# Masked queries on VectorE alone, and feature-map exponentials given to ScalarE only when their buffer is free

## The chip, the cores and the metric

The kernel runs on one core of a Trainium2 chip, as one launch. The metric is the device time of that launch in microseconds (us), the median of several runs. The core has five engines that each work through their own queue of instructions in order and wait for each other by semaphores: PE (TensorE, matrix multiply), DVE (VectorE), ACT (ScalarE), POOL (GpSimd) and SP (SyncE, which here only issues DMAs).

## The reference

A residual stream `x` of 2048 tokens by 512 features in bfloat16 goes through four layers, A, B, A, B. Each layer adds its output to `x`:

```
x = x + A(layernorm(x));  x = x + B(layernorm(x));  x = x + A(layernorm(x));  x = x + B(layernorm(x))

A: q, k, v = x@wq, x@wk, x@wv           32 heads of 16, 4 segments of 512 tokens
   for each segment s:
     a_dot = softmax(q_s k_s^T * 0.25 + causal mask) v_s
     pq    = phi(q_s);  a_mem = pq M / (pq z + 1e-6)
     o_s   = g * a_mem + (1 - g) * a_dot          g = sigmoid(beta)
     M, z += phi(k_s)^T v_s, sum(phi(k_s))        phi(t) = t + 1 where t > 0, else exp(t)
   return o @ wo
B: q, k, v = split(x @ wqkv);  return softmax(q k^T * 0.25) v @ wo       32 heads of 16, all 2048 tokens
```

Layer B's attention has 32 heads x 2048 x 2048 scores, each of which needs an exponential; there are two such layers. Layer A's is within segments and causal, and adds two feature maps `phi` per segment.

## The kernel before, in words

**An order written at build time.** A Python class (`Builder`) runs once when the program is built. It keeps a planner (`Sched`) with a clock for each engine, `sc.t[...]`. Each instruction that is added gets a planned end from a duration and a rate in its call (`ns`, `gap`), and semaphore waits are worked out from what it reads and writes. The planner's clocks decide what is added next, so a changed duration or engine changes the order of everything after it. On the chip nothing is decided: each engine executes its list in order.

**Steps.** The main loop (`attention`) is a series of steps (1407 before the change). A step takes three banks of scores (`take_banks`): a bank is 128 keys by 512 queries of one head, one bank of PSUM. `unit` adds the PE matmuls that make the scores, and one ACT instruction (L1289) that exponentiates all three banks, 1,536 columns wide, from PSUM into `pT` in SBUF. Two sets of three PSUM banks alternate. Two steps later `pv_step` multiplies `pT` with the values into an accumulator in PSUM bank 6. When a group of banks is done (one half of the heads of a 128-feature chunk, for one segment of queries), `finish` has DVE divide by the sums (L1341, a reciprocal, and L1349, which writes `ob`); PE can't start the next group's accumulation before that.

**Exponentials on DVE.** `dx_pick` takes some banks out of layer B's groups. Their scores go to PSUM bank 7; DVE copies and scales them (`dx_first`, L932), and a chain of five DVE instructions for a pair of banks (`dx_chain`, L957 to L968) makes the exponential with integer and float16 arithmetic into `dxo` (some of the tiles lie in `KA`, `QA` and `VA`, once these are no longer needed). A bank is picked only if the planner's DVE clock isn't too late.

**Background.** Everything else (layer norm, projections, memory, output projections) is written as generators ("tasks"). Each `yield` names what must be met (a flag, a DMA landed, a step reached), and the PE and DVE time of what follows; `background` runs what fits between steps. `keep_busy` adds dummy matmuls with zero weights where PE has little to do.

**Masked queries.** Heads have 16 features, and the score matmuls contract over 32 rows, so that two heads share a row block. For each group the queries are multiplied with a column of zeros and ones that keeps one head of the two: `qm = q * par` (`select`, L1197, 128 x 512 bfloat16). There are six `qm` buffers. The engine is chosen by

```
eng = "dve" if late or isA or any(h.kind == "A" for h in self.sel) else "pool"
```

so POOL makes those of layer B when the group is selected ahead of time and no layer-A group is selected: 86 of 160. They are made in pairs (the two groups of a chunk), normally when the second group of the pair before begins.

**Feature maps.** `phi(src, ...)` takes `[128 x 1024]` of keys or queries at a time. ACT writes `exp(src)` into the buffer `amem` (L618, 24 times), and two steps later or more DVE does `max(src, 0) + 1` (L620) and the minimum of that and `amem` (L621). There is one such buffer, which the memory part also uses (L707 writes it, and a DMA transpose reads it). In the kernel before nothing in the planner holds the ACT instruction back: it is added as soon as the task comes to it, and ACT's queue waits there on a semaphore until the minimum of the call before has read `amem`.

Of the kernel before, what the change touches and what calls it, by code (L numbers as in the profile page):

```python
# [23 lines left out]
LAG = {"pe": 100, "act": 60, "dve": 60, "pool": 70, "sp": 50}  # L24
# [231 lines left out]

class Builder:
    NPU = 4
    LAG_M = 2
    LOOK, PV_TAKEN = 1, 1  # L260
    NQM = 6
# [26 lines left out]
    def alloc(self):  # L288
# [21 lines left out]
        self.rd = sb("rd", [P, 2, 16], f32)  # L310
        self.pT = sb("pT", [P, self.NPU, 3, 512], bf)
        self.qm = sb("qm", [P, self.NQM, 512], bf)
# [44 lines left out]
        self.b_rd = n1("rd", 2)  # L357
        self.b_pT = n1("pT", self.NPU * 3)
        self.b_qm = n1("qm", self.NQM)
# [255 lines left out]
    def phi(self, src, bsrc, dst, bdst):  # L615

        et = self.amem[:, :, :, :].rearrange("p a b c -> p a (b c)")
        self.op("act", lambda e: e.activation(et, src, ACT.Exp), reads=bsrc, writes=self.b_amem, ns=1023, gap=915)  # L618
        yield [("at", self.step + 2)], 0, 1130
        self.op("dve", lambda e: e.tensor_scalar(dst, src, 0.0, 1.0, op0=ALU.max, op1=ALU.add), reads=bsrc, writes=bdst, ns=430)  # L620
        self.op("dve", lambda e: e.tensor_tensor(dst, dst, et, ALU.min), reads=self.b_amem + bdst, writes=bdst, ns=690)  # L621
# [392 lines left out]
    def met(self, need):  # L1014
        def done(key):
            step, end = self.dma_at.get(key, (-9, 0.0))
            return self.bubble or self.forcing or self.step >= step + self.DMA_STEPS and end < self.sc.t["pe"] + self.DMA_LATE

        def ok(n):
            if n == "xT":  # L1020
                return len(self.xT_free) > 0
            if n == "xn":
                return done(("xn", self.rr.get("xn", 0) % 2))
            if n[0] == "dma":
                return n[1] in self.dma_at and done(n[1])
            if n == "pair":
                return len(self.dx_pairs) > 0
            if n == "slot":
                return len(self.dx_free) > 0
            if n[0] == "at":  # L1030
                return self.bubble or self.forcing or self.step >= n[1]
            return n == "cont" or n in self.flags
        return all(ok(n) for n in need)
# [124 lines left out]
    def select(self, late):  # L1158
        tail = self.sel[-2:]
        if not self.LOOK and len(self.sel) > 2 and self.seqA and self.seqA[0][0].L and all(g.kind == "B" and not g.pos for g in tail) and self.met(self.group_needs(self.seqA[0][0])):  # L1160

            for g in tail:
                self.sel.remove(g)
                self.qm_free.insert(0, g.qm)
            self.seqB.insert(0, tail)
        while len(self.qm_free) > 1:
            pair = None
            look = self.LOOK and self.wide

            at = next((i for i, g in enumerate(self.sel) if g.kind == "B" and g.e == 0 and not g.pos), len(self.sel)) if look else len(self.sel)  # L1170
            few = at <= 1 or not look and at == 2 and all(g.kind == "B" and g.total < 64 for g in self.sel)
            short = look and len(self.sel) == 2 and all(g.kind == "B" and g.total < 64 for g in self.sel)
            if self.seqA and (few or short) and self.met(self.group_needs(self.seqA[0][0])):
                pair = self.seqA.pop(0)
                if not few:
                    at = len(self.sel)
            elif self.seqB and at == len(self.sel) and (few or short or look and self.seqB[0][0].total == 64 and all(g.kind == "A" for g in self.sel)) and self.met(self.group_needs(self.seqB[0][0])):
                pair = self.seqB.pop(0)
                at = len(self.sel)
            elif short and self.seqB and self.met(self.group_needs(self.seqB[0][0])):  # L1180
                pair = self.seqB.pop(0)
                at = len(self.sel)
            elif not few and not short:
                return
            if pair is None and self.seqB and sum(len(g.banks) - g.pos for g in self.sel) <= 6 and self.split():
                pair = self.seqB.pop(0)
            if pair is None:
                return
            for i, g in enumerate(pair):
                g.qm = self.qm_free.pop(0)  # L1190
                isA = g.kind == "A"
                q = (self.QA[:, self.aslot(g.L, g.qseg), g.c, :] if isA else self.QB[:, g.qseg, g.c, :])
                bq = (self.b_QA[self.aslot(g.L, g.qseg)][g.c] if isA else self.b_QB[g.qseg][g.c])
                m = self.qm[:, g.qm, :]
                col = self.par[:, g.e:g.e + 1]
                eng = "dve" if late or isA or any(h.kind == "A" for h in self.sel) else "pool"
                self.op(eng, (lambda m, q, col: lambda e: e.tensor_scalar(m, q, col, 0.0, op0=ALU.mult, op1=ALU.add))(m, q, col),  # L1197
                        reads=[bq, self.b_par], writes=[self.b_qm[g.qm]], ns=690 if eng == "pool" else 345, gap=650 if eng == "pool" else 260)
                self.sel.insert(at + i, g)
# [26 lines left out]
    def unit(self, n, items, dx):  # L1226
        u = n % 2
        al = self.new_alloc()
        slot = n % self.NPU
        entries, first_mm, second_mm = [], [], [[], [], []]  # L1230
        for i, (g, (what, r)) in enumerate(items):
# [21 lines left out]
            if what == "k2":  # L1253

                self.held.append((n + self.LAG_M, g.mate, "k2m", r, slot, i, width))
                if r == 3:
# [274 lines left out]
```

## Time and profile before

| | |
|---|---|
| median of 3 runs (lowest, highest) | 1989.19 us (1988.31, 1990.08) |
| the profiled execution's own time | 1988.43 us |
| its span, first to last instruction | 1986.6 us |
| busy: ACT, PE, DVE, POOL | 1932.9, 1750.7, 1654.1, 88.8 us |
| ACT exponentials of scores (L1289) | 1407, 1904.6 us |
| masked queries on POOL / on DVE (L1197) | 86, 81.2 us / 74, 22.9 us |
| exponentials of feature maps (L618) | 24, 26.2 us |
| mean granted TensorE clock | 0.996 |

Busy time is the union of an engine's instructions; an instruction's recorded duration overlaps the next one's by some tens to hundreds of nanoseconds, so busy time divided by the count is what one more instruction costs an engine that is never idle. "Idle before" is idle time of an engine just ahead of a group of instructions, with what ended most of it.

### The profile page before, as it was taken

How to read it: one execution, taken by the hardware profiler on the slowest of the kernel's cores; microseconds unless marked ns; L12 is line 12 of the kernel's file. 1: busy time of each engine (PE TensorE's matmuls, PEld its weight loads, DVE VectorE, ACT ScalarE, POOL GpSimd, SP SyncE). 2: the span in 40 equal slices, each digit the busy share in tenths (PEclk: the TensorE clock that was granted, in tenths of full speed). 3: DMA queues.
4: the chain of work that ended last, by engine and by line, in shares of the span. 5: the costliest groups of instructions: out<-in, count | busy, mean ns of one | idle time of the engine just before them, and what ended most of it. 6: DMA issues, size and time to landing. Idle time of an engine off the chain costs nothing.

```text
span 1986.6 us, 62277 instructions
## 1 busy us (share of the span) xinstructions
PE 1750.7 (88%) x27733; PEld 934.8 (47%) x27733; DVE 1654.1 (83%) x2960; ACT 1932.9 (97%) x1447; POOL 88.8 (4%) x132
## 2 busy tenths in 40 slices
PE   8998898888888888888888889988888888888888
PEld 5554454444554445444454445544444444444444
DVE  5655554599899998899879996489999999999997
ACT  7899999999999999999999999999999999999998
POOL 0000001100010000000000000001000000000000
PEclk9999999999999999999999999999999999999999
DMA  5211111000000001100101011000000000000000
GB/s 155 36 21 34 28 21 26 4 10 18 16 10 15 5 15 21 18 15 5 18 19 16 5 24 22 15 5 7 15 5 4 5 15 5 5 7 14 6 5 12
DMA packets 100942, 34.82 MB, mean 18 GB/s; under 512 B 93504, under 2 KB 100160, under 8 KB 100672
## 3 DMA queue, kind: packets, MB, share of 16 engines
q1 hardware_dynamic: 100672, 30.83, 8.0%
q8 instruction: 217, 3.56, 0.8%
q14 instruction: 53, 0.43, 0.1%
HBM read 6.30 MB, written 2.10 MB: 4 GB/s over the span
## 4 chain that ended last, share of the span: by engine, by line
ACT 54%; issue 22%; PE 16%; DVE 8%; DMA 1%; SPq 0%; ACTq 0%; POOL 0%; DVEq 0%; POOLq 0%
ACT pT L1289 53%; PE ps L400 16%; ACT amem L618 1%; DVE dxo L968 1%; DMA oT<-ob 1%; DVE ob L1349 1%; DVE dxt L932 1%; DVE VA L960 0%; DVE dxz L960 0%; DVE VA L957 0%; DVE rd L1341 0%; DVE dxz L957 0%; DVE KA L932 0%; DVE phq L621 0%; DVE VB L427 0%
## 5 line engine op out<-in xcount | busy, mean ns | idle before, releaser
L1289 ACT ACTIVATE pT<-ps 128x1536 bf16<-128x1536 f32 x1407 | 1904.6, 1628 | 34.2 <-PE ps L400 31.1
L400 PE MATMUL ps<-qm,KB 32*128 32x512 bf16 x4096 | 524.8, 386 | 171.0 <-ACT pT L1289 143.1
L400 PEld LDWEIGHTS ps<-VB,pT 128*128 128x128 bf16 x14316 | 460.4, 96 | 297.4 <-issue 217.4
L400 PE MATMUL ps<-VB,pT 128*128 128x34 bf16 (+1 forms) x14316 | 576.4, 186 | 20.9 <-DVE ob L1349 12.1
L400 PEld LDWEIGHTS ps<-qm,KB 32*128 32x128 bf16 x4096 | 133.9, 91 | 498.1 <-ACT pT L1289 443.5
L400 PE MATMUL ps<-wB,zero 128*128 128x512 bf16 x1079 | 343.7, 380 | 0.0
L932 DVE TENSOR_SCALAR dxt<-ps 128x512 uint32<-128x512 f32 x260 | 178.1, 685 | 21.0 <-PE ps L400 16.5
L1197 POOL TENSOR_SCALAR qm<-QB,par 128x512 bf16<-128x512 bf16 x86 | 81.2, 946 | 1745.0 <-PE ps L400 1463.8
L400 PE MATMUL ps<-qm,KA 32*128 32x128 bf16 (+2 forms) x1536 | 86.7, 254 | 25.3 <-ACT pT L1289 22.4
L400 PE MATMUL ps<-VB,dxo 128*128 128x51 bf16 (+1 forms) x1552 | 102.7, 186 | 0.9 <-DVE dxo L968 0.7
L400 PE MATMUL ps<-VA,pT 128*128 128x51 bf16 (+1 forms) x2560 | 101.0, 187 | 2.6 <-DVE ob L1349 2.0
L400 PEld LDWEIGHTS ps<-VA,pT 128*128 128x128 bf16 x2560 | 91.9, 96 | 10.8 <-DVE ob L1349 5.5
L932 DVE TENSOR_SCALAR KA<-ps 128x512 uint32<-128x512 f32 x128 | 87.7, 685 | 9.8 <-PE ps L400 7.6
L932 DVE TENSOR_SCALAR QA<-ps 128x512 uint32<-128x512 f32 x129 | 88.5, 686 | 8.0 <-PE ps L400 6.2
L400 PE MATMUL ps<-tri,ident 128*128 128x256 bf16 (+1 forms) x640 | 94.1, 255 | 0.0
L960 DVE TENSOR_TENSOR dxz<-dxz 128x1024 f16<-128x1024 f16 (+1 forms) x131 | 89.5, 683 | 0.7
L964 DVE TENSOR_TENSOR dxz<-dxz 128x1024 f16<-128x1024 f16 (+1 forms) x131 | 89.2, 681 | 0.4
L960 DVE TENSOR_TENSOR VA<-VA 128x1024 f16<-128x1024 f16 (+1 forms) x131 | 88.4, 675 | 0.6
L964 DVE TENSOR_TENSOR VA<-VA 128x1024 f16<-128x1024 f16 (+1 forms) x131 | 88.4, 675 | 0.5
L968 DVE SCALAR_TENSOR_TENSOR dxo<-dxt,dxz 128x1024 int16<-128x1024 uint16 (+1 forms) x66 | 80.6, 1221 | 0.2
L400 PEld LDWEIGHTS ps<-qm,KA 32*128 32x128 bf16 x1536 | 38.6, 92 | 88.6 <-ACT pT L1289 48.8
L968 DVE SCALAR_TENSOR_TENSOR dxo<-dxt,VA 128x1024 int16<-128x1024 uint16 (+1 forms) x66 | 78.7, 1192 | 0.2
(125 smaller groups left out, 1625.9 us busy)
## 6 DMA issues: line engine op xcount, KB each, us to landing
out_dram<-x SPq DMA_DIRECT2D x8, 256.0 KB, 2.1
x<-in_A_x_dram SPq DMA_DIRECT2D x3, 512.0 KB, 8.6
wB<-in_B_wqkv_dram SPq DMA_DIRECT2D x1, 1536.0 KB, 12.7
oT<-ob SPq DMA_TRANSPOSE x63, 2.5
xT<-xn SPq DMA_TRANSPOSE x60, 2.4
x<-in_A_x_dram SPq DMA_DIRECT2D x4, 128.0 KB, 2.2
wA<-in_A_wk_dram SPq DMA_DIRECT2D x1, 512.0 KB, 4.1
wA<-in_A_wq_dram SPq DMA_DIRECT2D x1, 512.0 KB, 5.4
```

What stands on the lines that cost most here:

```text
L400: self.sc.add("pe", lambda e: e.matmul(out, lhsT, rhs, start=start, stop=stop, skip_group_check=True), reads=reads, banks=[(bank, "w", all ...
L618: self.op("act", lambda e: e.activation(et, src, ACT.Exp), reads=bsrc, writes=self.b_amem, ns=1023, gap=915)
L932: self.op("dve", lambda e: e.tensor_scalar(d, o, SCALE * LOG2E * 65536, 126.0 * 65536, op0=ALU.mult, op1=ALU.add), writes=self.dx_writes(" ...
L960: self.op("dve", lambda e: e.tensor_tensor(z, z, z, ALU.mult), reads=bz, writes=bz, ns=ns[0])
L964: self.op("dve", lambda e: e.tensor_tensor(z, z, z, ALU.mult), reads=bz, writes=bz, ns=ns[0])
L968: self.op("dve", lambda e: e.scalar_tensor_tensor(ob, hi, 128.0, z, op0=ALU.mult, op1=ALU.add), reads=bt + bz, writes=self.dx_writes("out" ...
L1197: self.op(eng, (lambda m, q, col: lambda e: e.tensor_scalar(m, q, col, 0.0, op0=ALU.mult, op1=ALU.add))(m, q, col), reads=[bq, self.b_par] ...
L1289: self.sc.add("act", (lambda dst, src: lambda e: e.activation(dst, src, ACT.Exp, scale=SCALE))(dst, src), writes=self.b_pT[slot * 3 + i:sl ...
L1349: self.op("dve", lambda e: e.tensor_tensor(ob, src[:, :, 0:16], rb, ALU.mult), reads=[br] + bsrc, writes=[self.b_ob[oi][g.e]], bank=bk, al ...
```

## The change

Two edits, on otherwise the same code. First, `select` gives all masked queries to DVE: the 86 that POOL made move there, and the planner now charges them to its DVE clock (its choice of `ns` and `gap` by engine stays in the line). POOL keeps the set-up and 32 small memsets. Second, `phi` gets a new `yield` ahead of the ACT instruction: the task waits until all that read or last wrote `amem`, and what last wrote the source, is planned to end no later than 40 ns after the planner's ACT clock (`LAG["act"]` is 60, `PHI_LATE` 100); DMAs among these are not counted. While it waits, the next tasks and steps go on being added.

```
 class Builder:
     NPU = 4
+    PHI_LATE = 100
...
     def phi(self, src, bsrc, dst, bdst):

         et = self.amem[:, :, :, :].rearrange("p a b c -> p a (b c)")
+        yield [("free", self.b_amem, bsrc)], 0, 0
         self.op("act", lambda e: e.activation(et, src, ACT.Exp), reads=bsrc, writes=self.b_amem, ns=1023, gap=915)
         yield [("at", self.step + 2)], 0, 1130
...
+            if n[0] == "free":
+                used = [o for b in n[1] for o in b.reads.values()] + [b.last_write for b in n[1] + n[2] if b.last_write is not None]
+                return self.bubble or self.forcing or all(o.is_dma or o.end + LAG["act"] < self.sc.t["act"] + self.PHI_LATE for o in used)
...
-                eng = "dve" if late or isA or any(h.kind == "A" for h in self.sel) else "pool"
+                eng = "dve"
                 self.op(eng, (lambda m, q, col: lambda e: e.tensor_scalar(m, q, col, 0.0, op0=ALU.mult, op1=ALU.add))(m, q, col),
                         reads=[bq, self.b_par], writes=[self.b_qm[g.qm]], ns=690 if eng == "pool" else 345, gap=650 if eng == "pool" else 260)
```

Because the planner's clocks change, the order changes too. Counted in the two built programs: the score exponentials on ACT go from 1406 of 1,536 columns and one of 512 to 1408 of 1,536 and one of 1,024; the banks that DVE exponentiates go from 517 to 510; `keep_busy` matmuls from 1079 to 1080; the DMAs stay at 195.

## The prediction

> **What bounds the kernel now.** I read the engines' busy times first, then what ACT waited for, then ACT by stage, then the rows of the moved work.
>
> From the page: the engines, and the costliest groups.
>
> ```profile
> PE 1750.7 (88%) x27733; PEld 934.8 (47%) x27733; DVE 1654.1 (83%) x2960; ACT 1932.9 (97%) x1447; POOL 88.8 (4%) x132
> ...
> L1289 ACT ACTIVATE pT<-ps 128x1536 bf16<-128x1536 f32 x1407 | 1904.6, 1628 | 34.2 <-PE ps L400 31.1
> ...
> L1197 POOL TENSOR_SCALAR qm<-QB,par 128x512 bf16<-128x512 bf16 x86 | 81.2, 946 | 1745.0 <-PE ps L400 1463.8
> ```
>
> ACT is busy for all but 1986.6 - 1932.9 = 53.7 us of the span. One exponential of three banks costs it 1904.6 / 1407 = 1.354 us; the recorded 1.628 overlaps the next. POOL has 86 masked queries and hardly anything else.
>
> What ACT waited for:
>
> ```profile
> ACT pT L1289 <- PE ps L400: 31.1, 61, 1.7
> ...
> ACT amem L618 <- DVE phk L621: 1.9, 2, 1.3
> ...
> ACT amem L618 <- DVE phq L621: 1.7, 2, 1.4
> ```
>
> Waits for the feature maps' buffer are 3.6 us, in four places. Three stand together, in ACT's timeline from 195 to 208 us (start, duration, and in brackets the idle time before):
>
> ```profile
> 196.95 1.06 ACT L618 ACTIVATE amem<-phk 128x1024 bf16<-128x1024 bf16 x1 [1.28 <-DVE phk L621]
> ...
> 201.26 1.06 ACT L618 ACTIVATE amem<-QA 128x1024 bf16<-128x1024 bf16 x1 [0.57 <-DVE phk L621]
> ...
> 206.39 1.06 ACT L618 ACTIVATE amem<-QA 128x1024 bf16<-128x1024 bf16 x1 [1.39 <-DVE phq L621]
> ```
>
> Busy time by stage (DVE, ACT and POOL are the third to fifth pair):
>
> ```profile
> 130.00:290.00 160.00, 140.94 (x2150) 79.63 (x2148) 84.70 (x198) 155.94 (x119) 9.40 (x20) 1.00 0.16 26
> 290.00:1300.00 1010.00, 892.80 (x14227) 486.10 (x14223) 835.64 (x1514) 991.45 (x738) 43.83 (x68) 0.99 0.08 15
> 1300.00:1978.00 678.00, 592.46 (x9532) 293.74 (x9530) 652.49 (x1034) 676.48 (x504) 32.18 (x26) 1.00 0.03 7
> ```
>
> So ACT idles 4.1 us from 130 to 290 (3.2 of it the waits above), 18.6 us up to 1300, 1.5 us after that, where DVE is at 96% too. What is left lies before 130 us and after 1978 us, where the change alters nothing: the first POOL query starts at 131 us, and the two programs add the same work in the same order up to step 115 (at 197 us). Hence the time moves only by ACT's own work and by those three stretches.
>
> **1. ACT's work.** The planner gives DVE seven exponential banks fewer, 510 for 517, and ACT gets them: two more instructions of three banks, 2 x 1.354 = 2.7 us, and the last, partial one has two banks for one, (1.354 - 0.49) / 2 = 0.43 us with 0.49 as the one-bank row's 0.765 us less its measured overlap. Sum **+3.1 us**, with nothing to hide it, ACT being the bound. Every other ACT count is the same.
>
> **2. The waits for `amem`.** In the order before, these four exponentials are added in the very step of the minimum (L621) that frees the buffer. In the new order the three at 197 to 206 us come one, one and two steps after it, so one, one and two ACT instructions of 1.354 us lie between; the waits were 1.28, 0.57 and 1.39. I take **-3.2 us**. The fourth (0.30 us at 109 us) is unchanged, so it stays. Bounds: -3.2, and 0 if PE can't bring the scores sooner. I take the first: PE is 88% busy there (140.94 of 160) and its waits for ACT show that it is ahead. The other exponentials come up to 16 steps later than before; the DVE minimum, the memory matmuls and their DMA transposes behind them come later with them, and the count of steps that ran short of ready banks is 54 for 55, so no attention work starves.
>
> **3. The queries on DVE.** The nearest row is the same operation there, 64 of layer A's:
>
> ```profile
> L1197 DVE TENSOR_SCALAR qm<-QA,par 128x512 bf16<-128x512 bf16 x64 | 19.7, 350 | 0.9 <-ACT QA L425 0.8
> ```
>
> 19.7 / 64 = 0.308 us, times 86 = +26.5 us of DVE. Against that, seven banks fewer: each is 0.685 us (L932) and half a chain, (0.685 + 0.689 + 0.418 + 0.687 + 1.229) / 2 = 1.85, together 2.54, so -17.8 us. And DVE loses what POOL costs it now. Of the 143 DVE instructions that overlapped one of POOL's queries, the excess over their groups' medians is 4.1 us in all, for instance here, where this form's mean is 1.230:
>
> ```profile
> 1541.69 1.63 DVE L968 SCALAR_TENSOR_TENSOR dxo<-dxt,dxz 128x1024 int16<-128x1024 uint16 x1
> ```
>
> Net +26.5 - 17.8 - 4.1 = **+4.6 us of DVE**, of some 330 us in which it idles. Does it wait for the `qm` buffer, with all of DVE's queue behind it? The 74 that DVE makes already waited 0.9 us in all, none of it on PE. In time the term is nothing by cover: what hides it is that PE runs ahead of ACT, one set of three PSUM banks. That cover is thin at one place, the end of a group:
>
> ```profile
> PE ps L400 <- DVE ob L1349: 14.1, 26, 1.5
> ```
>
> PE waits there for DVE to empty the accumulator, and where it waits 0.8 us or more, ACT idles after it. After 1300 us only the 0.98 us wait there cost ACT anything (0.45 us); four of about 0.51 and one of 0.74 cost nothing. A pair of queries (0.62 us of DVE) now stands two or three steps ahead of nearly every first end of a pair of groups, some 43 times. Bounds: +43 x 0.62 = +26.7 us if each passes through to ACT, and -4.1 us if the stretching by POOL was what held it up. I take **0**, nearest to what the order shows: in the three steps up to a group's end after step 195, the new order has 5.3 DVE instructions where the old has 5.4, since the planner charges the queries and gives something else up. I keep -4.1 for the low end, and a third of 26.7, about +9, for the high one, since the planner puts two thirds of such load elsewhere: net 4.6 of 26.5 is even less.
>
> Here the Trainium skill ("SBUF — State Buffer", section "SBUF: two separate sides") has a rule: VectorE and GpSimd take a shared port pair as an exclusive lock for a whole instruction, and the loser fully blocks. If every POOL query had blocked DVE for its shortest recorded time, 0.692 us, DVE would gain 86 x 0.692 = 59.5 us. The trace shows 4.1 on DVE and 81.2 - 59.5 = 21.7 us of stretching on POOL, so by the trace POOL is mostly the loser, and the sum keeps 4.1.
>
> **4. A forced chain.** One more group ends with its DVE exponentials not yet made (two times for once, at step 941), so that PE waits for one or two chain instructions of 0.7 to 1.2 us. The one before, near 1146 us, was followed by no ACT gap over 0.2 us. I take **+0.3**, bounds 0 and +1.5.
>
> **Sum:** +3.1 - 3.2 + 0 + 0.3 = +0.2 us. The profiled execution took 1988.43 us, 0.76 below the median of its runs; it becomes 1988.6, and the median 1989.19 becomes **1989.4 us**. A measurement of this kernel can tell about 0.2%, 4 us, from no change.
>
> **The rivals.**
> *Same, by cancelling (the forecast), chance 0.50.* +3.1 of exponentials against -3.2 of waits. Within it lies the case that the wait only changes its name, from `amem` to PE: -3.2 becomes 0, +3.4, 1992.6.
> *Group ends hold ACT up (slower), 0.27.* The 0.62 us ahead of a group's end passes the PSUM cover. Price: 0.62 us for each end that lets it through. With the +0.2 it is over 4 us from the seventh of 43 on (0.2 + 7 x 0.62 = 4.5); a third of them gives +9, 1998. For it: DVE at 96% after 1300 us, where the number of DVE banks from step 950 on is the same as before (243) and 24 queries come on top. Against it: the order's counts in part 3, and the waits of 0.51 us that cost nothing.
> *DVE is freed from POOL, and the reshuffled middle packs better (faster), 0.23.* The 4.1 us come off DVE just ahead of group ends, and come off ACT's 18.6 us of idle time between 290 and 1300. Price: -4.1, so +0.2 - 4.1 = -3.9, 1985.3; another 2 us of the 18.6 gives 1983. For it: ACT gaps at 406.6, 1043, 1077, 1126 and 1427 us stand about 6.5 us behind a pair of POOL queries. Against it: so does the end of a group anyway, and POOL pairs at 1345 and 1445 us have no gap behind them.
> By the lock rule of "SBUF — State Buffer" alone DVE would win 59.5 us, which would point to this rival; its trace price is the 4.1.
> *The change doesn't do what it says* isn't one: the order of the new program has no query on POOL, and the exponentials are moved.
>
> **How the numbers follow.** The order of everything after 197 us is reshuffled, and ACT's 20 us of idle time there is made of some 40 gaps of about half a microsecond; a few more or fewer make 2 to 4 us. Hence 0.50 within 4 us of no change, 0.27 above, 0.23 below. The range reaches to the group-end case's +9, 1998, and the packing case's 1983, and leaves about 0.1 out on either side; the likeliest case's own range is 1985.5 to 1993.
>
> **What would show it.** Right: ACT's L1289 at 1409 instructions and about 1907.7 us; no wait of L618 on L621 near 200 us, one of 0.3 near 109; POOL with 50 instructions; L1197 on DVE at 160 and about 49 us; DVE some 5 us busier, with no stretched L968. Wrong on the slow side: PE's wait for `ob` well above 14.1 us with ACT's wait for PE above 31.1. Wrong on the fast side: both below. A second way to be wrong: ACT's wait for PE grows by 3 us just where `amem`'s is gone.

## The result and the profile after

The changed kernel takes **2000.95 us** (median of 4 runs, 1997.29 to 2005.84); the kernel before, beside it, 1988.75. The ratio is 1.0058, with a 95% interval of 1.0044 to 1.0073: some 12 us slower, where 1989.4 us and no change were forecast. The profiled execution is the slowest of the four, 2005.84 us with a span of 2003.9, 17.3 us over the span before.

The engines, and the exponentials' row, in the page of the changed kernel (L1294 is the former L1289):

```profile
PE 1703.7 (85%) x27315; PEld 934.5 (47%) x27734; DVE 1655.6 (83%) x3029; ACT 1937.2 (97%) x1449; POOL 8.7 (0%) x46
...
L1294 ACT ACTIVATE pT<-ps 128x1536 bf16<-128x1536 f32 x1409 | 1909.2, 1633 | 50.3 <-PE ps L401 48.1
```

ACT does 4.3 us more, and the other 13.0 us of the span are ACT waiting. (Some 400 matmul records are missing here, so PE's busy time isn't compared.) What ACT and then PE waited for; L620 is the exponential of the feature maps, L1202 the masked query:

```profile
ACT pT L1294 <- PE ps L401: 48.1, 81, 2.2
...
ACT amem L620 <- DVE phq L623: 0.3, 1, 0.3
```

```profile
PE ps L401 <- DVE ob L1354: 11.3, 21, 1.3
...
PE ps L401 <- DVE qm L1202: 8.2, 8, 1.8
```

The waits for the feature maps' buffer are gone but for the 0.3 us that was to stay. The group ends are no worse (11.3 us, 14.1 before). But PE now waits 8.2 us for masked queries, where the kernel before has 2.1, and ACT's wait for PE has grown from 31.1 to 48.1. The line of the kernel before:

```profile
PE ps L400 <- DVE qm L1197: 2.1, 2, 1.1
```

By stage:

```profile
130.00:290.00 160.00, 139.84 (x2171) 81.55 (x2201) 88.61 (x213) 158.12 (x120) 0.00 (x0) 0.99 0.15 26
290.00:1300.00 1010.00, 862.13 (x13830) 480.71 (x14019) 826.49 (x1539) 980.18 (x729) 3.69 (x16) 0.98 0.08 15
```

From 130 to 290 us ACT idles 1.9 us for 4.1; from 290 to 1300, 29.8 for 18.6. The granted clock, the first figure after the busy times, is lower. Its records show 16 stretches in which half of PE's clock was granted (half-clock stretches below) between 20 and 1975 us, 61 us together; before there were five, 17 us. Summed over these stretches alone, first of the kernel before, then of the changed one:

```profile
sum 17.06, PE 16.95 PEld 7.45 DVE 10.71 ACT 12.72 POOL 0.00; mean PE 3.39 PEld 1.49 DVE 2.14 ACT 2.54 POOL 0.00
sum 61.44, PE 57.83 PEld 27.68 DVE 48.66 ACT 46.12 POOL 0.24; mean PE 3.61 PEld 1.73 DVE 3.04 ACT 2.88 POOL 0.02
```

ACT idles in them for 17.06 - 12.72 = 4.3 us before and 61.44 - 46.12 = 15.3 us after, while PE is recorded busy nearly throughout. So 11.0 of the 13.0 us that ACT waits longer in the profiled execution stand in half-clock stretches.

One place shows how a wait for a query and the half clock hang together. ACT, DVE and PE around 1680 us, three timelines of the changed kernel:

```profile
1681.69 2.79 ACT L1294 ACTIVATE pT<-ps 128x1536 bf16<-128x1536 f32 x2 [1.43 <-PE ps L401]
1684.97 1.45 ACT L1294 ACTIVATE pT<-ps 128x1536 bf16<-128x1536 f32 x1 [0.49 <-PE ps L401]
1687.16 4.13 ACT L1294 ACTIVATE pT<-ps 128x1536 bf16<-128x1536 f32 x3 [0.74 <-PE ps L401]
```

```profile
1678.24 1.22 DVE L970 SCALAR_TENSOR_TENSOR VA<-QA,VA 128x1024 int16<-128x1024 uint16 x1
1679.37 0.61 DVE L1202 TENSOR_SCALAR qm<-QB,par 128x512 bf16<-128x512 bf16 x2
```

```profile
1677.62 0.39 PE L401 MATMUL ps<-qm,KB 32*128 32x512 bf16 x3 [0.25 <-ACT pT L1294]
1679.77 0.39 PE L401 MATMUL ps<-qm,KB 32*128 32x512 bf16 x1 [1.76 <-DVE qm L1202]
```

The pair of queries stands behind the exponentials in DVE's queue; PE needs the first one in the next step and waits 1.76 us; ACT runs dry for 1.43. And the windows before and after:

```profile
1677.40:1680.80 3.40, 1.36 (x17) 0.61 (x18) 3.11 (x6) 2.86 (x3) 0.00 (x0) 1.00 0.00 0
1680.80:1687.60 6.80, 6.31 (x76) 3.19 (x77) 6.06 (x12) 4.68 (x4) 0.00 (x0) 0.50 0.00 0
```

PE is busy for 1.36 of 3.40 us, and in the 6.8 us after that its clock is half, ACT idling there again. Not every half-clock stretch begins so: of the 16, two follow 3.4 us in which PE waited more than 1 us for a query (at 829 and 1678 us), and five follow 3.4 us with a wait of 0.56 to 1.34 us for the end of a group (`ob`).

### The profile page after: what moved, and what is told of

The parts are those of the page before. It is cut to its first block, busy times and chain, and to the rows that moved or that the text cites. A ratio compares the mean times of both kernels' runs of the same rounds, so it can differ in the third digit from the quotient of the medians.

```text
span 2003.9 us, 61698 instructions
## 1 busy us (share of the span) xinstructions
PE 1703.7 (85%) x27315; PEld 934.5 (47%) x27734; DVE 1655.6 (83%) x3029; ACT 1937.2 (97%) x1449; POOL 8.7 (0%) x46
## 4 chain that ended last, share of the span: by engine, by line
ACT 48%; issue 20%; PE 17%; DVE 13%; DMA 1%; SPq 0%; ACTq 0%; POOL 0%; DVEq 0%; POOLq 0%
ACT pT L1294 48%; PE ps L401 17%; DVE dxo L970 2%; DVE dxt L934 1%; ACT amem L620 1%; DVE ob L1354 1%; DVE dxz L959 1%; DMA oT<-ob 1%; DVE VA L970 1%; DVE dxz L962 1%; DVE VA L962 1%; DVE VA L966 1%; DVE KA L934 1%; DVE QA L934 1%; DVE dxz L966 0%
## 5 line engine op out<-in xcount | busy, mean ns | idle before, releaser
L1294 ACT ACTIVATE pT<-ps 128x1536 bf16<-128x1536 f32 x1409 | 1909.2, 1633 | 50.3 <-PE ps L401 48.1
L401 PE MATMUL ps<-qm,KB 32*128 32x512 bf16 x4096 | 516.9, 389 | 207.8 <-ACT pT L1294 179.7
L401 PE MATMUL ps<-VB,pT 128*128 128x51 bf16 (+1 forms) x14344 | 580.9, 187 | 18.6 <-DVE ob L1354 9.8
L401 PEld LDWEIGHTS ps<-qm,KB 32*128 32x128 bf16 x4096 | 128.4, 91 | 507.7 <-ACT pT L1294 453.0
L401 PE MATMUL ps<-wB,zero 128*128 128x512 bf16 x769 | 262.8, 388 | 12.8 <-issue 2.6
L934 DVE TENSOR_SCALAR dxt<-ps 128x512 uint32<-128x512 f32 x255 | 174.8, 685 | 14.7 <-PE ps L401 11.9
L401 PE MATMUL ps<-VB,dxo 128*128 128x34 bf16 (+1 forms) x1528 | 102.0, 187 | 3.2 <-DVE dxo L970 3.1
L970 DVE SCALAR_TENSOR_TENSOR VA<-QA,VA 128x1024 int16<-128x1024 uint16 (+1 forms) x65 | 78.0, 1200 | 1.4 <-PE ps L401 1.2
L970 DVE SCALAR_TENSOR_TENSOR dxo<-KA,dxz 128x1024 int16<-128x1024 uint16 (+1 forms) x65 | 77.4, 1191 | 1.4 <-PE ps L401 1.3
L970 DVE SCALAR_TENSOR_TENSOR dxo<-dxt,dxz 128x1024 int16<-128x1024 uint16 (+1 forms) x65 | 78.0, 1200 | 0.3 <-DVE VA L964 0.2
## 6 DMA issues: line engine op xcount, KB each, us to landing
wB<-in_B_wqkv_dram SPq DMA_DIRECT2D x1, 1536.0 KB, 11.9
```

The lines of the kernel that those rows point to most:

```text
L401: self.sc.add("pe", lambda e: e.matmul(out, lhsT, rhs, start=start, stop=stop, skip_group_check=True), reads=reads, banks=[(bank, "w", all ...
L934: self.op("dve", lambda e: e.tensor_scalar(d, o, SCALE * LOG2E * 65536, 126.0 * 65536, op0=ALU.mult, op1=ALU.add), writes=self.dx_writes(" ...
L970: self.op("dve", lambda e: e.scalar_tensor_tensor(ob, hi, 128.0, z, op0=ALU.mult, op1=ALU.add), reads=bt + bz, writes=self.dx_writes("out" ...
L1294: self.sc.add("act", (lambda dst, src: lambda e: e.activation(dst, src, ACT.Exp, scale=SCALE))(dst, src), writes=self.b_pT[slot * 3 + i:sl ...
```

## The experiments

### Each part alone, and each order with the other engine

The planner makes two things of the queries' move: another engine, and another order of everything. These four kernels take the two apart, and the feature maps from both. In the last two the planner charges one engine and the instruction goes to another, so that the order stays to the instruction that of the kernel named.

The feature-map wait alone:

```
-                eng = "dve"
+                eng = "dve" if late or isA or any(h.kind == "A" for h in self.sel) else "pool"
```

> The feature-map wait alone; queries chosen by the old rule. The order of the program differs from before only in steps 110 to 130. Theory 'queries' (the loss comes from the queries' move): 1985.5 to 1989 us, the three waits near 200 us gone (-3.2 us) and five or so half-clock stretches as before. Rival 'feature maps' (the later exponentials cost it): 1997 or more.

Measured: 1984.02 us (1982.92 to 1984.99), ratio 0.998 (0.997 to 0.9989). This part wins 4.3 us, and the kernel with it alone is the fastest measured here. Its stage from 130 to 290 us:

```profile
130.00:290.00 160.00, 139.40 (x2164) 81.29 (x2192) 86.08 (x202) 157.85 (x119) 9.44 (x20) 0.99 0.15 26
```

ACT idles 2.1 us there for 4.1, although two new waits for PE, of 0.70 and 0.49 us, stand at 200 and 202 us.

The queries' move alone, the kernel before with:

```
-                eng = "dve" if late or isA or any(h.kind == "A" for h in self.sel) else "pool"
+                eng = "dve"
```

> The queries' move alone, without the feature-map wait. Theory 'queries': 1999 to 2006 us, with a dozen or more stretches at half clock and PE waiting some 8 us for qm. Rival 'feature maps': 1988 to 1993 us.

Measured: 2003.24 us, ratio 1.0078 (1.0063 to 1.0093), 12 half-clock stretches, PE waits 8.2 us for queries. So the loss, 14.9 us, comes with the queries' move and the order that it makes.

The changed kernel's order, 84 queries executed by POOL:

```
+                real = "dve" if late or isA or any(h.kind == "A" for h in self.sel) else "pool"
-                self.op(eng, ...
+                self.op(real, ..., plan=eng)
```

> The changed kernel's order to the instruction, planned as if DVE made the queries, but 84 of them are executed by POOL. Theory 'queue' (DVE makes the queries late, PE waits for them and its clock falls): 1987 to 1992 us, PE no longer waits for qm, about five half-clock stretches. Rival 'order' (the new order itself leaves PE idle in more stretches, whoever makes the queries): 1998 us or more, a dozen half-clock stretches.

Measured: 1995.94 us, ratio 1.0039 (1.0026 to 1.0052), nine half-clock stretches, PE's wait for queries 3.6 us. Between the two theories: 5.0 us of the changed kernel's 2000.95 go with the engine (the two intervals overlap a little, 1.0052 and 1.0044; PE's wait shows the direction), but in the same order without the engine 11.9 us remain against the feature-map wait alone.

The order before, all queries executed by DVE:

```
-                self.op(eng, ...
+                self.op("dve", ..., plan=eng)
```

> The order of the kernel before to the instruction, planned as if POOL made the 86 queries, but DVE executes them, unplanned. Theory 'queue': 1996 to 2006 us, PE waits 8 us or more for qm. Rival 'order': 1988 to 1992 us.

Measured: 1996.51 us, ratio 1.0042 (1.0027 to 1.0057), PE waits 4.3 us for queries. The time lies in the range of theory 'queue', though the wait is half of the 8 us expected; eleven half-clock stretches go with it. The execution on DVE costs 8.2 us here, where the planner didn't reckon with it. Both theories hold a part.

### Is it the half clock?

If idle PE loses its clock and that starves ACT, dummy matmuls should help. In the first two kernels 406 of them are added in the given order, without telling the planner:

```
+        if g is not None and g.npv and self.wide and self.banks[6].writes and self.sc.streamed(
+                max(self.sc.t["pe"], self.sc.t["act"] - 1330), 3413) < self.EXTRA:
...
```

Here `EXTRA` is 0.6, and the lines left out add one matmul of zeros into bank 6, with no planned time.

> The changed kernel's order to the instruction, with 406 more dummy matmuls of zeros (0.213 us of streaming each) put in where the planner's coverage of PE is under 0.60, which the planner isn't told of. Theory 'clock' (idle PE lets its clock fall to half for 3.4 us, and that is what starves ACT): under six half-clock stretches for 16, and 1988 to 1994 us. Rival 'symptom' (PE's waits starve ACT, and the half clock only goes along with them): 1998 us or more, whatever the clock shows.

> The control: the feature-map wait alone, with 406 dummy matmuls more by the same rule. It had three half-clock stretches, so theory 'clock' has little to win here: 1982 to 1986 us. If the dummies themselves delay PE, 1988 us or more, and this is then the price to take off the run beside it.

Measured: on the changed kernel's order 2006.00 us, ratio 1.0092 (1.0069 to 1.0115); on the control 1992.21, 1.0023 (1.0014 to 1.0033). In the profiled executions the first has 4 half-clock stretches for 16, the control 2 for 3. The first became 5.1 us slower, the control 8.2: the dummies have a price, and with it both times lie above the ranges that theory "clock" gave without one.

The first kernel's four runs say more than their median. Two, at mean clocks of 0.996 and 0.997, took 2002.67 and 2002.79 us; the other two, at 0.991, took 2010.68 and 2009.21. So only two runs were nearly rid of the half clock. These two are 10.5 us behind the control; less the control's price of 8.2 us they would stand at 1994.5, some 6 us below the changed kernel (an estimate: the price may differ between the orders). So the half clock isn't all of the loss, and the pair can't say how much of it.

That it is a good part is seen where the instructions stay the same and only the clock differs. The 83 runs of the kernel before that were timed beside the experiments go from 1987.50 us on average at a mean clock of 0.997 (32 runs) to 1990.52 at 0.993 (3 runs). The ten runs of a kernel below (16 queries on POOL) go from 1990.08 us at 0.997 to 2001.00 at 0.990. The changed kernel's fastest run, 1997.29 us at 0.992, is 6.8 us behind the kernel before at 0.993, where the medians are 12.2 apart. So some 6 us of the 12 go along with the clock, an estimate from these runs.

The planner's own bound for dummies, which changes the order too:

```
-    FILL = 0.58
+    FILL = 0.70
```

> The changed kernel with the planner's own bound for dummy matmuls at 0.70 for 0.58 (1637 of them for 1080), which it plans, so that its order changes too and DVE gets six banks fewer (ACT +2.6 us). Theory 'clock': few half-clock stretches, 1990 to 1996 us. Rival 'symptom': 2001 us or more.

> The feature-map wait alone, with the bound at 0.70 (1623 dummies, three banks fewer on DVE, ACT +1.3 us). Theory 'clock': 1983 to 1988 us, no half-clock stretch left. Rival: the planned dummies crowd PE, 1989 us or more.

Measured: 1995.71 us (1.0036, 1.0023 to 1.0049) with the queries on DVE, 1991.98 (1.0019, 1.0010 to 1.0029) with the old choice of engine. The difference is 3.7 us, and ACT has three exponentials more in the first, 4.1 us. In these two orders the queries' move costs no more than its exponentials, where it cost 17 in the orders before. The first time lies in the range of theory "clock": one half-clock stretch (6.8 us) is left in its profile, and all five runs have a mean clock of 0.998 or 0.999. The second is a miss for that theory: four stretches are left where none was expected, and the planned dummies cost more than they win. Since the bound changes the order and the clock together, the pair doesn't tell these two apart; it does show that the move need not cost 17 us.

### Shaking the order

The planner's bounds were moved by 10 ns, one at a time, in kernels with and without the queries' move (both with the feature-map wait):

```
-    DX_BANK, DX_LATE, BG_BANK, DVE_LATE, DVE_LATE_LOW = 500, 4000, 200, 1200, 5000
+    DX_BANK, DX_LATE, BG_BANK, DVE_LATE, DVE_LATE_LOW = 500, 4000, 210, 1200, 5000
...
-    FILL_DVE = 300
+    FILL_DVE = 290
```

> The feature-map wait alone, reordered by moving one planner bound by 10 ns (background matmuls for a bank up to 210 ns late, for 200): 1407 ACT exponentials of scores as in the unshaken one. Theory 'lottery' (the loss of the changed kernel's order is in good part the luck of one order among many): 1984 to 1993 us, several us away from 1984.0. Rival 'systematic' (the order with queries on DVE is worse as such): 1983 to 1986 us, like the unshaken one.

> The changed kernel shaken by the same 10 ns, with 1409 exponentials as in the unshaken one. Lottery: 1991 to 2003 us, and the gap to its partner without the queries' move anywhere from 3 to 17 us. Systematic: 1999 to 2004 us, a gap of 14 us or more.

> The feature-map wait alone, shaken by another bound (DVE filled up to 290 ns past a bank's readiness, for 300), 1408 exponentials. Lottery: 1984 to 1994 us. Systematic: 1984 to 1987 us (one exponential more is 1.4 us).

> The changed kernel shaken by the same bound, 1412 exponentials, four more than its partner (5.4 us). Lottery: 1994 to 2006 us, a gap of 5 to 17 us. Systematic: 2003 to 2008 us, a gap of 17 us or more.

| | old choice of engine | all on DVE | difference |
|---|---|---|---|
| unshaken | 1984.02 | 2000.95 | 16.9 |
| BG_BANK 210 | 1996.30 | 1993.94 | -2.4 |
| FILL_DVE 290 | 1992.72 | 2004.70 | 12.0 |

With the same 1407 exponentials on ACT the first shake costs the left column 12.3 us; with the same 1409 it gives the right one 7.0. "Systematic" falls: the difference is anything from -2.4 to 16.9 us. (1996.30 us is above the range of "lottery" too.) The clock moves along: in the profiled executions the left column has 3, 8 and 10 half-clock stretches from top to bottom, the right one 16, 7 and 9.

Is it the shake alone? Two kernels without either part of the change, the kernel before with `BG_BANK` at 210, and with another bound 10 ns up:

```
-    DVE_FIN, DX_FIN = 600, 9000
+    DVE_FIN, DX_FIN = 610, 9000
```

> The kernel before, shaken by the 10 ns of the earlier runs (background matmuls for a bank up to 210 ns late); 1407 exponentials on ACT, as unshaken. Theory 'lucky order': 1994 to 2002 us, the loss of the shake without either part of the change. Rival (the shake hurts only with the feature-map wait): 1986 to 1991 us.

> The kernel before, shaken by another 10 ns (DVE's lateness allowed near a group's end 610 for 600); 1406 exponentials, one fewer. Theory 'lucky order': 1990 to 2000 us although ACT has 1.4 us less to do. Rival: 1985 to 1989 us.

Measured: 2000.33 us (1.0060, 1.0043 to 1.0078) and 1987.66 (0.9995, 0.9986 to 1.0004). The first alone loses as much as the whole change did, 12 us, with ten half-clock stretches, in which ACT idles 10.2 us for 4.3. Its wait, beside the 31.1 us of the unshaken kernel:

```profile
ACT pT L1289 <- PE ps L400: 40.0, 74, 2.3
```

The second lost nothing: a miss for "lucky order" as I put it. Its order departs at step 759 only, the first one's at 428. So not every shake costs, but a 10 ns one can cost all that the change did.

### Which queries on DVE cost the time

Two kernels keep an order to the instruction and give POOL only the pairs that are needed one or two steps after they are made: 16 queries in the changed kernel's order, 8 in the order before.

```
+                real = "dve" if late or isA or any(h.kind == "A" for h in self.sel) or self.step not in (244, 245, 254, 255, 263, 264, 520, 521, 565, 566, 601, 602, 741, 742, 995, 996, 1175, 1176) else "pool"
...
+                self.op("pool" if eng == "pool" and self.step in (245, 255, 264, 1100) else "dve", ..., plan=eng)
```

> The changed kernel's order to the instruction; only 16 queries, the pairs whose first is needed one or two steps after it is made, are executed by POOL, the others by DVE. Theory 'wait' (PE waits for queries that stand at the end of DVE's queue): all of the 5 us comes back, 1994 to 1998 us. Rival 'load' (26 us more for DVE delay everything a little): 1999 us or more.

> The order of the kernel before to the instruction; DVE executes the queries but for 8, made one or two steps ahead of their use at steps 245 to 264 and 1100, which stay on POOL. Theory 'wait': 1988 to 1991 us, for 1996.5 with all on DVE. Rival 'load': 1994 us or more.

Measured: 1993.99 us (1.0032, 1.0019 to 1.0046) and 1997.03 (1.0042, 1.0028 to 1.0056). In the changed kernel's order the median with 16 on POOL is 2.0 us below that with 84, the intervals overlapping. PE's wait for queries, and ACT around the place shown above:

```profile
PE ps L402 <- DVE qm L1204: 3.7, 3, 1.6
```

```profile
1663.81 9.92 ACT L1296 ACTIVATE pT<-ps 128x1536 bf16<-128x1536 f32 x7
1674.02 17.57 ACT L1296 ACTIVATE pT<-ps 128x1536 bf16<-128x1536 f32 x13 [0.29 <-PE ps L402]
```

The gaps of 1.43, 0.49 and 0.74 us are gone. But so is the half clock at this place in this execution. With 84 queries on POOL, in the same order, there was a half-clock stretch from 1675.3 to 1682.1 us, and of the three gaps only the first has shrunk:

```profile
1676.43 1.45 ACT L1296 ACTIVATE pT<-ps 128x1536 bf16<-128x1536 f32 x1 [0.21 <-PE ps L402]
1678.59 1.45 ACT L1296 ACTIVATE pT<-ps 128x1536 bf16<-128x1536 f32 x1 [0.70 <-PE ps L402]
1680.77 9.51 ACT L1296 ACTIVATE pT<-ps 128x1536 bf16<-128x1536 f32 x7 [0.74 <-PE ps L402]
```

So the first gap is in the main the query's, and the others go with the half clock. The ten runs with 16 on POOL agree: six, at clocks of 0.993 to 0.997, took 1990.08 to 1995.55 us, and four, at 0.989 to 0.991, took 1998.49 to 2001.00, hardly less than the changed kernel's 2000.46 and 2001.43 at 0.990 and 0.988. What the 16 queries bring back is mostly a higher clock in most runs.

In the order before, keeping the urgent ones on POOL brought nothing back, though PE's wait for queries fell from 4.3 us to 2.1, as in the kernel before: there it isn't those waits. Theory "load" forecast this time; how the 24 us of DVE work that the planner left no room for cost it isn't shown further.

The engine in the shaken orders:

> The changed kernel shaken by 10 ns (1993.9 us), in that order to the instruction, with 84 queries executed by POOL. If execution on DVE costs the same in every order: 1986 to 1989 us. If it cost nothing in this order: 1992 us or more.

> The feature-map wait alone shaken by 10 ns (1996.3 us), in that order (one dummy matmul more), with all queries executed by DVE, unplanned. If execution on DVE costs the same in every order: 2001 to 2006 us. If not: 1994 to 1999 us.

Measured: 1994.39 us (1.0028, 1.0018 to 1.0037), beside 1993.94 with DVE; and 2004.09 (1.0083, 1.0067 to 1.0099), beside 1996.30 with POOL. Unplanned, the execution on DVE costs 7.8 us, as it did in the other order (8.2). Planned, it costs 5 to 7 by the medians in one order, and nothing in the other.

## Why the prediction was wrong

**ACT's work (+3.1)**: right in its count, 1409 score exponentials; their busy time is 1909.2 us (1.355 each), 4.6 more than before, where about 1907.7 was forecast. POOL was left with 46 instructions, not the 50 that the prediction names.

**The waits for `amem` (-3.2)**: right, measured alone at -4.3. The three waits went, and a third of the gain did turn into waits for PE (0.70 and 0.49 us). Where the rest of the 4.3 comes from isn't shown; the profiled run had three half-clock stretches for five.

**The queries on DVE (0)**: the failed step. The sum of DVE's time was near: +4.6 us forecast, its busy time rose by 1.5, and the stretched instructions are gone (the longest L970 takes 1.226 us, before 1.675). The cover was wrong. I looked for the thin place at the ends of groups, where waits fell to 11.3 us; it was at the query itself. I argued that DVE's own 74 queries never waited for PE, and didn't ask who waits for them. POOL had hardly anything else in its queue; at the place shown the query stands in DVE's queue behind two exponential instructions of 0.68 and 1.22 us, and where the group begins in the next step, PE waits. Measured: 6.1 us more of PE's waits, and 5 to 7 us of time by the medians in this order, of which at most 3 us are left between runs at the same clock (at 0.990: 2000.46 us with all on DVE, 1997.41 with 84 on POOL, 2001.00 with 16).

**How the numbers follow (2 to 4 us for the reshuffle)**: the other failed step, and the larger term. I put the scatter of the order down to some 40 gaps of half a microsecond each, as if they fell by chance around the gaps before, and the sum has no term for PE's clock. Measured, the order alone moves the time by far more: three of the four kernels without the queries' move whose order was shaken by 10 ns came out 8.7 to 12.3 us slower than their unshaken partner, one 0.8 faster. The changed kernel's order, with queries on POOL, is 11.9 us behind the feature-map wait alone; 3.1 of that is ACT's work by the forecast. And much of the order's effect goes along with the half clock, of which the changed kernel has 16 stretches for five. The trace of one kernel doesn't show how its order compares with its neighbours. What could be seen is that the change moves the order of everything after step 115, for a DVE load that nets to nearly nothing.

**What I misread in the trace before.** Of the five gaps that I put down to POOL, the two at 406.6 and 1126 us stand at half clock, or nearly (402.9 to 406.3 and 1123.1 to 1126.5 us). The other three, at 1043, 1077 and 1427 us, don't: each follows a wait of PE of 0.88 to 0.98 us for a group's end. A group's end can also bring the half clock about: the longest such wait, 1.46 us, ends at 808.3 us. The windows of the kernel before around 810 us:

```profile
805.70:809.10 3.40, 1.60 (x43) 1.08 (x40) 2.72 (x6) 3.33 (x3) 0.00 (x0) 1.00 0.00 0
809.10:812.50 3.40, 3.40 (x31) 1.45 (x29) 1.63 (x2) 1.45 (x1) 0.00 (x0) 0.50 0.50 43
```

ACT does 1.45 us of work in those 3.4. The 0.99 of granted clock in the row of 290 to 1300 us told of such stretches (there are five in all), and no rival was built on it. The Trainium skill ("TensorE: Matmul & The Clock Gate", section "What's actually happening") says that the matrix engine's clock is halved after an idle window of about 3.4 us, that the window runs freely, and that it opens again after a busy one. The trace agrees on the length (the stretches are 3.41 us or twice that), and on the window's running freely: counted from the first half-clock stretch of the kernel before, the others begin 17, 136, 228 and 309 times 3.413 us later. It shows that the window needn't be idle: PE was busy for 1.60 and 1.36 us of 3.40 ahead of the two shown, and no single gap of PE in the kernel before after 20 us is longer than 1.9 us. A window that runs freely would also fit that one program's runs differ by 11 us along with their clock: the same dip of PE can fall into one window or be split between two. That this is the reason isn't shown.

**The rivals.** "Group ends hold ACT up" forecast the direction and 1998 us. In total PE's waits there got shorter (11.3 us for 14.1), so its price of 0.62 us an end isn't what was paid. But five of the 16 half-clock stretches begin behind such a wait, one of five before, so the ends have a part by way of the clock. "DVE is freed from POOL" found its stretched instructions gone, and no gain of time shows from it.

What stays open: how the loss divides into half clock and plain waits. In the profiled executions, 11.0 of the 13.0 us of ACT's added waiting stand in half-clock stretches. By the changed kernel's and the kernel before's runs at nearly the same clock, some 6 of the 12 us go along with it (the profiled execution has the lowest clock of the four). The changed order with queries on POOL and the feature-map wait alone differ by 11.0 us of ACT's idle time, 6.0 of it in half-clock stretches. No run held the clock still without adding work to PE, so that the half clock's own share isn't shown by an experiment.

## What to carry to other kernels

Where a planner lays out the program, a change is three things: the work, the engine and a new order. Measure them apart by executing a fixed order with the other engine, and shake the order by a harmless constant before believing a difference of its size; here 10 ns moved the time by anything from 12 us up to 7 us down. When a producer moves to a busier engine's queue, look for the consumers that need it in the very next step: in the changed kernel's order, taking 16 of 84 queries off DVE brought back by the medians what taking off all did. Before a gap is put down to the wait that ended last, put it beside the records of the granted clock; and compare runs at the same clock, since here a lower clock went with up to 11 us more between runs of one program. And the part that was worth having, the wait of the feature maps, shows only when it is run alone: 1984.02 us.

## What the runs showed of the hardware

The half-clock stretches of one execution lie on one grid. In each of the twenty traces they begin whole multiples of 3.413 us apart, to within 3 ns; each lasts one such window or two. So what can be compared is how busy PE was in the windows of that grid. In the changed kernel the nine least busy windows at full clock, 41 to 59% busy in the records, were all followed by half clock; the next, at 61%, wasn't, and seven others between 61 and 83% were (some matmul records are missing there, so these shares are a little low). In the kernel before, windows of 47, 60, 64, 64 and 66% were followed by half clock, and two of 59 and 60% weren't. So here a window in which PE is busy for two thirds can bring half clock, and the records give no sharp bound.

ACT, which needs PE's scores, was busy for 75% of the half-clock stretches in both kernels (12.72 of 17.06 us and 46.12 of 61.44), and for 97% of the whole span.

The number of such stretches differs from run to run of one program: the changed kernel's four runs had mean clocks of 0.992, 0.990, 0.988 and 0.984, and took 1997.29, 2000.46, 2001.43 and 2005.84 us.
